# First stage of a fused transform and SwiGLU kernel: input rises loaded in halves, placements in two-bank PSUM tiles, folds of two sets in one instruction, odd sums ahead of the value weights

## The chip, the cores and the metric

The kernel runs on one core of a Trainium2 chip. The metric is the device time of one execution in microseconds, median of several runs. A core has five engines with a queue of their own: TensorE (PE in the profile; its weight loads are PEld), VectorE (DVE), ScalarE (ACT), GpSimd (POOL) and SyncE (SP), which here only issues transfers. Matmul results land in PSUM, eight banks of 128 x 512 float32; everything else lives in SBUF.

## What is computed

```python
def _attn_ref(x):                       # x: 8 x 3008 x 256
    X = np.fft.fft(x, axis=1)
    X = np.fft.fft(X, axis=2)
    return X.real.astype(np.float32)

def _moe_ref(x, w_gate, w_val, w_out):  # x: 24064 x 256, d_ff 1536
    g = x @ w_gate
    silu = g * (1.0 / (1.0 + np.exp(-g)))
    val = x @ w_val
    return (silu * val @ w_out).astype(np.float32)
```

The real part of the two-dimensional transform of each of the eight batches goes, row by row, through a SwiGLU block. Inputs and the output are float32.

## The kernel before

**The long part.** The 256-point transform along the width is folded into the weights: the tables CD and SDt (cosines and sines) times the raw weights give Wp and Wq, and Wm is Wq with signs (`double`, and `weight_op` for the later thirds). The transform along the sequence gives for each batch two tables of coefficients, Pt (even) and Qt (odd), 512 columns to a tile. A "unit" is a tile and one of twelve slices of d_ff: products g (gate) and v (value) of Pt with Wp, of Qt with Wq and of Qt with Wm, silu on ACT, a product on VectorE (line 1053, and line 1074 for the mirrored rows), and later the product with Wo (line 1279). A planner (`Sched`) takes an estimated duration and a due time for each of these operations and writes out one order for each engine; the change leaves its costs and due times as they are. Its PSUM slots are three banks "g", three "v" and two "o". A unit holds its v bank until the mirrored product of line 1074 has read it, so that unit k+3 takes the bank of unit k.

**The first stage**, which the change rewrites, is an order written out by hand, in which the first batch is transformed and the first third of the weights is made, so that units can start. On each engine the order of the program is the order of execution; waits between engines are derived from which tile regions are read and written.

- Loads. Rows of the first batch that rise and that fall in index are paired. Part A has four sets of 128 pairs (tile XA: sets 0 to 3 rising, 4 to 7 falling), part C two sets of 120 in two half-partition groups (tile XC0). SP issues the rises of A in one transfer (line 261), two falls of A (264), the rises of C (267) and the four falls of C (270), which wait until ACT has cleared XC0 (292). ACT issues the other two falls. Row 0 comes from POOL's queue (404), as do all weights (`load_w`, 394): the gate weights' first third at 8.32 us, the others later.
- Warm-up. 48 matmuls of a zero tile with itself (line 306), eight more after the placements (472).
- Tables. POOL writes index tiles (iota), `turns` (364) and the placing matrices putA and putC; VectorE compares putA (355), computes `angles` (368) and `magnitude` (372); ACT makes the sine and cosine table Tab, CD and SDt.
- Placing. A float32 matmul with putA (or putC) turns the order of the rising rows of a set around, into one PSUM bank for each set (438).
- Folding. `cross` (447) adds the falling rows, reversed, to sets 0 and 1, `cross_halves` (451, 452) does so for sets 2 and 3 and for C in two halves; the second half is added in place in PSUM and shares a column with what the first reads. `half_fold` (460) then gives even and odd sums, `ends` (455) single columns. POOL's `fold_d` (497) gives the even and odd sums of sets 0 and 1, and the odd one of sets 2 and 3, for which ACT first copies the PSUM halves out (543). ACT casts the even sums to bf16 (500), POOL adds the odd ones (570).
- First products. `half_folded` (488) and `folded_c` (493) multiply the sums with Tab into the accumulators acc[0] (even) and acc[1] (odd), a bank each for two halves q. `row0` (628) adds single rows, `even_copy` (517) copies half q=0 to SBUF, and `first_puts` (646) forms Pt and Qt from the two halves on VectorE. `first_w` (505) makes the first third of Wp and Wq; its casts (508) run on ACT, but for the value weights' Wp, which VectorE casts. `turn_signs` (345 to 347) are three tiny VectorE instructions whose result POOL uses some ten units later.

Of the kernel before, what the change touches and what calls it, by code (L numbers as in the profile page):

```python
# [19 lines left out]
def kernel(  # L20
# [8 lines left out]
    nc = tc.nc  # L29
# [49 lines left out]
    psG = Slots("psG", 3, space=bass.MemoryType.PSUM)  # L79
    psV = Slots("psV", 3, space=bass.MemoryType.PSUM)  # L80
    psO = Slots("psO", 2, space=bass.MemoryType.PSUM)
# [39 lines left out]

    def up_block(b, j, n):
        return rows_at(b, 2 * j - 1, [[2 * D, n], [R * D, 4], [1, 2 * D]])
# [137 lines left out]
    q.dma_start(out=XA3[:, 0:4, :], in_=up_block(0, 1, P))  # L261
# [4 lines left out]
    def rises_c(eng):  # L266
        eng.dma_start(out=XC3[:, 0:2, :], in_=rows_at(0, 2 * (P + 1) - 1, [[2 * D, 64], [2 * R * D, 2], [R * D, 2], [1, 2 * D]]))
# [18 lines left out]
    nc.gpsimd.iota(putA, pattern=[[-LA, NA], [1, LA]], base=JA - 1, **iota)  # L286
# [16 lines left out]
    for i in range(4):  # L303
        ps = psO.tile([P, T], F32, name="o")
        for j in range(12):
            nc.tensor.matmul(ps[:, 0:P], sel, sel, start=True, stop=True)
# [48 lines left out]
    vts(putA, putA, scalar1=pcol, scalar2=None, op0=Alu.is_equal)  # L355
# [50 lines left out]
    pts(putC, putC, scalar1=pcol, scalar2=1.0, op0=Alu.is_equal, op1=Alu.mult)  # L406
    nc.gpsimd.memset(sel[0:1, :], 1.0)
# [22 lines left out]
    weigh_ce()  # L430
    opposite(0)

    def place(X, put, n, pools):
        pss = []
        for a in range(n):
            pool, nm = pools[a % len(pools)]
            ps = pool.tile([P, 2, D], F32, name=nm)
            nc.tensor.matmul(ps.rearrange("p q d -> p (q d)"), put, X[:, a].rearrange("p q d -> p (q d)"),
                             start=True, stop=True)
            pss.append(ps)  # L440
        return pss

    def falling(X, pss, a):
        return (X[:, 7 - a] if len(pss) == 4 else X[:, 2 + a])[:, ::-1]
# [1320 lines left out]
```

## Time and profile before

| | |
|---|---|
| time, median of 3 runs (lowest to highest) | 597.55 us (597.2 to 597.58) |
| time of the profiled execution | 597.77 us |
| its span | 596.0 us, 12394 instructions |
| busy: PE, DVE, ACT, POOL | 590.9, 568.6, 553.6, 533.5 us |
| granted TensorE clock | 1.00 in every stretch |
| VectorE, 20 to 25 and 25 to 30 us | 4.73 and 4.58 us busy of 5 |

The profile is one execution. A timeline row gives start, duration, engine, line, output and input tiles, shape and count; rows of the same kind are merged, and the duration then runs from the first start to the last end. Matmuls are pipelined, so a merged row is longer than its matmuls' starts are apart, by the tail of the last. A bracket at the end of a row tells how long the engine was idle before it and who released it. SPq and ACTq rows are issues of transfers, not the transfers. The view of transfers lists, for each queue, packets, megabytes and the share of 16 engines' time; q1 is SP's queue, q10 ACT's, q0 POOL's.

### The profile page before, as it was taken

How to read it: one execution, taken by the hardware profiler on the slowest of the kernel's cores; microseconds unless marked ns; L12 is line 12 of the kernel's file. 1: busy time of each engine (PE TensorE's matmuls, PEld its weight loads, DVE VectorE, ACT ScalarE, POOL GpSimd, SP SyncE). 2: the span in 40 equal slices, each digit the busy share in tenths (PEclk: the TensorE clock that was granted, in tenths of full speed). 3: DMA queues.
4: the chain of work that ended last, by engine and by line, in shares of the span. 5: the costliest groups of instructions: out<-in, count | busy, mean ns of one | idle time of the engine just before them, and what ended most of it. 6: DMA issues, size and time to landing. Idle time of an engine off the chain costs nothing.

```text
span 596.0 us, 12394 instructions
## 1 busy us (share of the span) xinstructions
PE 590.9 (99%) x4014; PEld 390.6 (66%) x4014; DVE 568.6 (95%) x1062; ACT 553.6 (93%) x1071; POOL 533.5 (90%) x491
## 2 busy tenths in 40 slices
PE   9999999999999999999999999999999999999997
PEld 6456676666666666666666666666666666666686
DVE  9989999999999999999999999999999999999993
ACT  8768989999998899899999999999999999999995
POOL 9979999999999999999899998999889868687782
PEclk9999999999999999999999999999999999999999
DMA  9976772756244255285125122054121103202212
GB/s 251 161 222 229 185 235 71 194 165 222 82 149 126 73 139 137 68 273 159 54 82 168 37 64 63 19 152 143 46 63 37 47 19 88 67 28 63 60 54 81
DMA packets 61070, 68.17 MB, mean 114 GB/s; under 512 B 6744, under 2 KB 48668, under 8 KB 61006
## 3 DMA queue, kind: packets, MB, share of 16 engines
q1 hardware_dynamic: 57422, 64.44, 36.1%
q0 software_dynamic: 3216, 2.36, 2.9%
q8 instruction: 31, 0.51, 0.4%
q10 hardware_dynamic: 368, 0.59, 0.3%
q14 instruction: 33, 0.27, 0.2%
HBM read 40.21 MB, written 35.43 MB: 127 GB/s over the span
## 4 chain that ended last, share of the span: by engine, by line
PE 96%; DVE 0%; ACT 0%; issue 0%
PE o L1279 41%; PE g L1015 27%; PE v L1015 21%; PE g L1453 2%; PE o L1453 2%; PE v L1279 1%; PE o L1501 1%; PE g L622 0%; PE o L622 0%; PE g L1279 0%; PE o L1582 0%; PE g L1650 0%; DVE Wp L508 0%; ACT es L1289 0%; DVE Qt L646 0%
## 5 line engine op out<-in xcount | busy, mean ns | idle before, releaser
L1226 POOL TENSOR_TENSOR hm<-sv 128x1024 bf16<-128x1024 f32 (+2 forms) x137 | 254.7, 1862 | 32.3 <-ACT sv L1202 12.9
L1218 DVE SCALAR_TENSOR_TENSOR sv<-es,v 128x512 f32<-128x512 f32 (+2 forms) x262 | 174.0, 670 | 5.9 <-PE v L1015 4.3
L1279 PE MATMUL o<-Wo,hm 128*128 128x256 bf16 (+1 forms) x1128 | 163.7, 273 | 0.0
L1279 PE MATMUL o<-Wo,hp 128*128 128x256 bf16 (+1 forms) x1104 | 161.1, 272 | 0.0
L1229 DVE TENSOR_TENSOR hp<-sp,v 128x512 bf16<-128x512 f32 (+2 forms) x228 | 151.6, 671 | 1.9 <-PE v L1015 1.1
L1279 PEld LDWEIGHTS <-hm 128*128 128x128 bf16 (+2 forms) x1140 | 111.9, 98 | 58.0 <-issue 0.6
L1279 PEld LDWEIGHTS <-hp 128*128 128x128 bf16 (+2 forms) x1140 | 111.8, 98 | 55.3 <-issue 0.3
L1202 ACT ACTIVATE sv<-g 128x512 f32<-128x512 f32 (+2 forms) x181 | 119.0, 675 | 3.6 <-PE g L1015 3.1
L1127 ACT ACTIVATE sp<-g 128x512 f32<-128x512 f32 (+2 forms) x181 | 112.1, 621 | 5.9 <-PE g L1015 4.0
L1015 PE MATMUL g<-Pt,Wp 128*128 128x512 bf16 (+2 forms) x288 | 107.5, 374 | 0.0
L1015 PE MATMUL v<-Pt,Wp 128*128 128x512 bf16 (+2 forms) x288 | 106.2, 375 | 0.2 <-DVE Wp L508 0.2
L1015 PE MATMUL g<-Qt,Wq 128*128 128x512 bf16 (+2 forms) x288 | 105.4, 375 | 0.1
L1088 ACT ACTIVATE v<-bc,w 128x512 f32<-128x512 bf16 (+2 forms) x139 | 100.3, 726 | 1.9 <-DVE sv L1218 1.0
L1152 DVE SCALAR_TENSOR_TENSOR es<-bc,w,v 128x512 f32<-128x512 bf16 (+2 forms) x135 | 97.9, 732 | 2.1
L1150 ACT ACTIVATE es<-v 128x512 f32<-128x512 f32 (+2 forms) x139 | 86.0, 621 | 3.2 <-PE v L1015 1.6
L1015 PEld LDWEIGHTS <-Wp 128*128 128x128 bf16 x576 | 56.3, 98 | 26.0 <-DVE Wp L508 1.0
L1015 PE MATMUL g<-Qt,Wm 128*128 128x512 bf16 (+2 forms) x195 | 73.1, 376 | 0.0
L1131 DVE SCALAR_TENSOR_TENSOR sg<-bc,w,g 128x512 f32<-128x512 bf16 (+2 forms) x93 | 67.3, 724 | 1.6 <-PE g L1015 1.4
L1235 POOL TENSOR_TENSOR hp<-sp,pp 128x512 bf16<-128x512 f32 (+1 forms) x46 | 57.2, 1245 | 8.0 <-ACT pp L1232 7.8
L1202 ACT ACTIVATE sv<-sg 128x512 f32<-128x512 f32 (+2 forms) x93 | 63.6, 695 | 0.5 <-DVE sg L1195 0.5
L1195 DVE SCALAR_TENSOR_TENSOR sg<-sg,g 128x512 f32<-128x512 f32 (+2 forms) x93 | 61.6, 663 | 0.2
L1015 PEld LDWEIGHTS <-Wq 128*128 128x128 bf16 x437 | 42.7, 98 | 27.5 <-issue 0.4
(218 smaller groups left out, 788.7 us busy)
## 6 DMA issues: line engine op xcount, KB each, us to landing
out_dram<-ev SPq DMA_DIRECT2D x96, 128.0 KB
XA<-in_x_dram SPq DMA_DIRECT2D x30, 256.0 KB
tA<-in_x_dram SPq DMA_DIRECT2D x28, 256.0 KB
XA<-tA SPq DMA_DIRECT2D x14, 512.0 KB
XC<-in_x_dram SPq DMA_DIRECT2D x28, 120.0 KB
tC<-in_x_dram SPq DMA_DIRECT2D x28, 120.0 KB
XC<-tC SPq DMA_DIRECT2D x6, 480.0 KB
bc<-br SPq DMA_DIRECT2D x19, 128.0 KB
```

The costliest lines, as they stand in the source:

```text
L1015: nc.tensor.matmul(ps[:, :n], Wt[:, gv, fs], src[:, :n], start=start, stop=stop, skip_group_check=True)
L1088: nc.scalar.activation(T_[kv][:, :w], bc[t][:, :w], AF.Copy, scale=w0[:, 1, f:f + 1])
L1127: nc.scalar.activation(sp_to()[:, :w], T_[kg][:, :w], AF.Silu)
L1131: nc.vector.scalar_tensor_tensor(T_[keg][:, :w], bc[t][:, :w], w0[:, 0, f:f + 1], T_[kg][:, :w], op0=Alu.mult, op1=Alu.add)
L1150: nc.scalar.activation(T_[kes][:, :w], T_[kv][:, :w], AF.Copy, scale=2.0 if on_pool(u) > 1 else 1.0)
L1152: nc.vector.scalar_tensor_tensor(T_[kes][:, :w], bc[t][:, :w], w0[:, 1, f:f + 1], T_[kv][:, :w], op0=Alu.mult, op1=Alu.add)
L1195: nc.vector.scalar_tensor_tensor(T_[kgm][:, :w], T_[keg][:, :w], 2.0, T_[kg][:, :w], op0=Alu.mult, op1=Alu.subtract)
L1202: nc.scalar.activation(sv()[:, f % 2, w - 1::-1, 1], T_[kgm if by_dve else kg][:, :w], AF.Silu)
L1218: nc.vector.scalar_tensor_tensor(sv()[:, f % 2, w - 1::-1, 0], T_[kes][:, :w], 2.0, T_[kv][:, :w], op0=Alu.mult, op1=Alu.subtract)
L1226: nc.gpsimd.tensor_tensor(hts_(t)[1][:, f - 1:f + 1, :w], sv()[:, :, :w, 1], sv()[:, :, :w, 0], op=Alu.mult)
L1229: nc.vector.tensor_tensor(hts_(t)[0][:, f, :wp], T_[ksp][:, :wp], T_[kv][:, :wp], op=Alu.mult)
L1279: nc.tensor.matmul(st["ps"][:n, j, :], hts[t][minus][:, f, c:c + n], Wo[:, f, :], start=(f == 0), stop=(f == nF - 1))
```

## The change

The rises of A are loaded in two halves (sets 0 and 1, then 2 and 3), each a transfer on SP; ACT issues falls 3 and 2, SP falls 1 and 0; the rises of C are two transfers as well; row 0 moves from POOL's queue to SP's, ahead of the falls of C. The warm-up has 28 matmuls in place of 48, and four after the placements in place of eight. The comparison for putA moves from VectorE to POOL, behind the first two `turns`, with its iota. PSUM is held in four tiles of two banks during the first stage, and the pools of the long part are opened after it. Cross sums, folds and ends take two sets at a time. The odd fold of sets 2 and 3 moves from POOL (and two ACT copies) to VectorE. On TensorE, all four even C products come ahead of the gate weights' products, and the odd sums with their rows ahead of the value weights'. The value weights' Wp is now cast by ACT, their Wq by VectorE. `turn_signs` stand at the end of the first stage; `row_signs`, the row of ones in sel, `weigh_ce` and `opposite(1)` change places.

```diff
-    psG = Slots("psG", 3, space=bass.MemoryType.PSUM)
...
+    first_ctx = ExitStack()
+    double_banks = [first_ctx.enter_context(tc.tile_pool(name=f"two{i}", bufs=1, space=bass.MemoryType.PSUM)) for i in range(4)]
+
+    def two_banks(i):
+        return double_banks[i].tile([P, 2, T], F32, name=f"b{i}")
...
-    q.dma_start(out=XA3[:, 0:4, :], in_=up_block(0, 1, P))
+    def rises_a(a):
+        q.dma_start(out=XA3[:, a:a + 2, :], in_=rows_at(0, R * a + 1, [[2 * D, P], [R * D, 2], [1, 2 * D]]))
...
+    def rises_c(a):
+        q.dma_start(out=XC3[:, a, :], in_=rows_at(0, 2 * P + 1 + R * a, [[2 * D, 64], [2 * R * D, 2], [1, 2 * D]]))
...
+    rises_a(0)
     nc.scalar.activation(w0[:, 0, 0:1], zero, AF.Silu)
     fall_a(3, nc.scalar)
-    fall_a(2, q)
-    fall_a(1, nc.scalar)
+    rises_a(2)
+    fall_a(2, nc.scalar)
+    fall_a(1, q)
     fall_a(0, q)
-    rises_c(q)
+    rises_c(0)
+    rises_c(1)
...
-    nc.gpsimd.iota(putA, pattern=[[-LA, NA], [1, LA]], base=JA - 1, **iota)
...
+    q.dma_start(out=XC0[NCR:64 + NCR + 1:64, 2:4, 0], in_=rows_at(0, 0, [[2 * R * D, 2], [R * D, 2], [1, D]]))
...
+    warm(28)
...
-    vts(putA, putA, scalar1=pcol, scalar2=None, op0=Alu.is_equal)
...
     turns(ti[0], kf, 0)
+    nc.gpsimd.iota(putA, pattern=[[-LA, NA], [1, LA]], base=JA - 1, **iota)
+    pts(putA, putA, scalar1=pcol, scalar2=1.0, op0=Alu.is_equal, op1=Alu.mult)
     turns(ti[1], kf, 1)
     more_iotas()
-    nc.gpsimd.dma_start(out=XC0[NCR:64 + NCR + 1:64, 2:4, 0],
-                        in_=rows_at(0, 0, [[2 * R * D, 2], [R * D, 2], [1, D]]))
...
-    nc.gpsimd.memset(sel[0:1, :], 1.0)
...
+    def cross_halves(to, ps, down):
+        d = len(ps.shape) - 3
+        m = (slice(None),) * (2 + d)
+        vtt(to, ps[m + (slice(1, P + 1),)], down[m + (slice(D - 1, P - 1, -1),)], op=Alu.add)
+        vtt(ps[m + (slice(P, D),)], ps[m + (slice(P, D),)], down[m + (slice(P, 0, -1),)], op=Alu.add)
...
+    (b01, ps01), (b23, ps23), (bC, psC) = (set_of_two(k) for k in (3, 1, 2))
+    for a in range(4):
+        place((b01, b23)[a // 2][:, a % 2], XA, putA, a)
+    warm(4)
+    cross(FA[:, 0:2], ps01, down01)
     load_w(0, (0,))
     fold_d(0, 0)
     load_w(0, (1,))
     fold_d(1, 0)
...
+    ends(Eh[:, 0:2], ps01, down01)
+    cross_halves(FA[:, 2:4, :, 1:P + 1], ps23, down23)
+    half_fold(0, EOA[0][1], FA[:, 2:4, :, 1:P + 1], ps23)
+    ends(Eh[:, 2:4], ps23, down23)
+    half_fold(1, EOA[1][1], FA[:, 2:4, :, 1:P + 1], ps23)
+    for a in range(2):
+        place(bC[:, a], XC0, putC, a)
+    start_acc(0, 0)
     half_cast(0, 0)
-    for a in range(2, 4):
-        nc.scalar.copy(FA[:, a, :, P + 1:D], psA[a][:, :, P + 1:D])
+    weigh_ce()
     half_cast(0, 2)
+    opposite(1)
...
     load_w(1, (0,))
-    fold_d(1, 2)
+    ptt(EOb[:, 1, 0:2], EOA[1][0], EOA[1][1], op=Alu.add)
...
+    for a in range(2):
+        cross_halves(FC[:, a], psC[:, a], downC[:, a])
+    half_fold(0, EB[:, 0], FC, psC)
+    half_fold(1, EB[:, 1], FC, psC)
+    ends(Ec0, psC, downC)
     folded_c(0, 0)
...
     folded_c(0, 1)
     od0 = even_copy(0)
...
+    first_ws = two_banks(1)
+    copies = [first_w(0, k, 1, first_ws[:, k]) for k in range(2)]
+    start_acc(1, 3)
     for a in range(2):
         folded_c(1, a, True)
-    half_folded(1, 0, False)
...
+    row_signs()
+    nc.gpsimd.memset(sel[0:1, :], 1.0)
...
     first_puts(0, od0, (0, 1))
-    for i in range(2):
-        row0(0, i, acc[1][i])
     copies[0]()
     copies[1]()
-    turn_signs()
-    od1 = even_copy(1)
-    copies += [first_w(1, k, k, psO.tile([P, T], F32, name="o")) for k in range(2)]
+    for i in range(2):
+        half_folded(1, 0, False, (i,))
+        row0(0, i, acc[1][i])
+        if i == 0:
+            od1 = even_copy(1)
+    second_ws = two_banks(2)
+    copies += [first_w(1, k, 1 - k, second_ws[:, k]) for k in range(2)]
     first_puts(1, od1, (0,))
     for c in copies[2:4]:
         c()
     first_puts(1, od1, (1,))
+    turn_signs()
     tmp_ctx.close()
+    first_ctx.close()
+
+    psG = Slots("psG", 3, space=bass.MemoryType.PSUM)
...
```

More of the change, by code (lines that the diff above doesn't have):

```diff
@@ L301, in more_iotas, with warm @@
             nc.gpsimd.iota(putC[:, pm - NCR:pm], pattern=[[-2 * LC, NC_], [2, LC]], base=2 * (NCR - LC) + hi, **iota)
[L303 to L306, printed above, removed]
+    idle = two_banks(0)
+    def warm(n):
+        for i in range(n):
+            nc.tensor.matmul(idle[:, 0, 0:P], sel, sel, start=True, stop=True)
+    warm(28)
     small = {}
```

85 lines of the change are left out of this document (20 added, 65 removed).

## The prediction

> **What bounds the kernel now.** I read the page first, then the chain that ended last in its first 22 us.
>
> ```profile
> span 596.0 us, 12394 instructions
> PE 96%; DVE 0%; ACT 0%; issue 0%
> ```
> ```profile
> 18.85 0.61 DVE Wp L508
> 19.50 0.58 PE v L1015 x2
> ```
>
> TensorE carries 96% of the chain, and the chain leaves it only here: at 19.50 the first value product has waited for the cast of the value weights on VectorE. Everything after 19.50 is matmul behind matmul in an order that the change leaves alone. So the change is worth what it does to the moment at which the unit products run without waiting, unless an engine that comes out of the first stage later then holds TensorE up. The profiled execution took 597.77 us: the span and 1.77 around it. That is 0.22 over the median, 597.55. I sum shifts against the span and apply them to the median. A difference under 0.2% (1.2 us) can't be told from no change in this kernel.
>
> **The placements.** The timeline from 0 to 40 us, columns start and duration:
>
> ```profile
> 1.04 5.30 PE L306 MATMUL o<-sel 128*128 128x128 bf16 x48 [1.04 <-DVE sel L258]
> 1.45 0.39 POOL L286 IOTA putA<- 128x128 f32 x1
> 2.13 2.86 POOL L364 TENSOR_SCALAR t<-kf,mM 128x377 int32<-128x377 f32 x4
> 3.50 0.61 DVE L355 TENSOR_SCALAR putA<-putA,pcol 128x128 f32<-128x128 f32 x1
> 6.13 1.36 PE L438 MATMUL g<-XA,putA 128*128 128x512 f32 x2
> 6.45 0.84 POOL L406 TENSOR_SCALAR putC<-putC,pcol 128x128 f32<-128x128 f32 x1
> 8.19 1.02 PE L438 MATMUL g<-XA,putA 128*128 128x512 f32 x2
> 9.05 1.02 PE L438 MATMUL v<-XA,putA 128*128 128x512 f32 x2
> 9.91 0.61 PE L472 MATMUL o<-sel 128*128 128x128 bf16 x8
> ```
>
> Twenty fewer idle matmuls at 5.30/48 = 0.11 end the warm-up at 4.1 instead of 6.1. The data of half the rises is 256 packets of 2 KB, and the transfer view up to 4 us has
>
> ```profile
> q1 hardware_dynamic: 266, 0.54, 46.0%
> ```
>
> so the first half is there at little over 4. The matrix putA moves to POOL: behind two of the four L364 (2.86/2 = 1.43, from about 1.85, since the iota ahead of them is gone) come its iota (0.39) and a comparison as L406 (0.84): 4.5, and 4.55 with the signal. The placements start there, and PE idles 0.45 us before them. A set takes 9.05-8.19 = 0.86.
>
> The warm-up shows a second thing: 48 matmuls took 0.11 each, and eight of the same form at 9.91 took 0.61 in all, under 0.08 each; the first placed pair took 1.36 where later ones took 1.02. So the array ran at about half rate until some 6.5 to 6.8. Before, the warm-up hid that; now placements run in it. Bounds: at full rate throughout, sets 0 and 1 are done at 4.55+1.72+0.17 = 6.45 and sets 2 and 3 at 8.15; at half rate until 6.8 they are done at 7.55 and 9.3. I take 7.4 and 8.95, near the row.
>
> The Trainium skill (TensorE: Matmul & The Clock Gate, Part 1) says that the array starts at half clock and is released after one busy window of about 3.4 us, and that these windows run freely. The rows agree with a slow start. If such a window must be filled without a gap, the count begins anew at 4.55 and the release falls between about 8 and 11.4, which by that page would be an estimate of 599 us; if a gap of 0.45 passes, my sum stands.
>
> **VectorE.**
>
> ```profile
> 7.35 0.56 DVE L372 TENSOR_SCALAR ra<-rr 128x754 int32<-128x754 int32 x1
> 7.84 0.68 DVE L447 TENSOR_TENSOR FA<-g,XA 128x510 f32<-128x510 f32 x1
> 8.44 0.68 DVE L447 TENSOR_TENSOR FA<-v,XA 128x510 f32<-128x510 f32 x1
> 9.25 0.43 DVE L451 TENSOR_TENSOR FA<-g,XA 128x256 f32<-128x256 f32 x1
> 9.71 0.43 DVE L452 TENSOR_TENSOR g<-g,XA 128x256 f32<-128x256 f32 x1
> 10.57 0.43 DVE L452 TENSOR_TENSOR v<-v,XA 128x256 f32<-128x256 f32 x1
> 10.91 0.41 DVE L460 TENSOR_TENSOR XA<-FA,g 128x256 f32<-128x256 f32 x1
> 11.71 0.41 DVE L451 TENSOR_TENSOR FC<-o,XC 128x256 f32<-128x256 f32 x1
> 12.15 0.43 DVE L452 TENSOR_TENSOR o<-o,XC 128x256 f32<-128x256 f32 x1
> 12.62 0.42 DVE L460 TENSOR_TENSOR EOf<-FC,o 128x256 bf16<-128x256 f32 x1
> 13.88 1.08 DVE L460 TENSOR_TENSOR EOf<-FC,o 128x256 bf16<-128x256 f32 x3
> ```
>
> From start to start, 510 elements cost 0.60 (7.84 to 8.44) and 256 cost 0.34 (10.57 to 10.91): 0.08 and 1.02 ns an element. A folding of two sets thus costs 1.12 for 1020 elements and 0.60 for 512: merging saves only 0.08 for each instruction gone. Where one needs the one before it, the pitch is 0.46 (9.25 to 9.71, which share a column) or 0.47 (12.15 to 12.62): 0.12 more.
>
> Without the 0.61 of L355, of which about 0.5 is queue, L372 ends at 7.4 and the cross sum of sets 0 and 1 runs from 7.45 to 8.57; with the ends VectorE is free at 8.65. It then waits for set 3 until 9.0. Sets 2 and 3: 0.72 and 0.73 (dependent), the even sum 0.60, ends 0.1, and the odd sum that comes over from POOL, 0.60: 2.75 against 2.46 before. The C part starts at 11.75, where it was 11.71. What the earlier placements give, the added odd sum takes.
>
> C part: 0.44 and 0.47 as at 11.71 to 12.62, the free pitch of 0.34 between the sets, so 0.44+0.34+0.44+0.47, then both sets' even sums in one (0.42+0.26 = 0.68): 14.12. Before, the second even sum ended at 13.88+0.42 = 14.30. That is 0.18 earlier, but both C sets now come at once.
>
> **TensorE behind it.**
>
> ```profile
> 14.00 0.59 PE L505 MATMUL g<-W,CD 128*128 128x512 bf16 x2
> 14.87 0.32 PE L493 MATMUL v<-Tab,EOf 128*128 128x378 bf16 x1
> 15.84 0.48 PE L488 MATMUL v<-Tab,EOb 128*128 128x377 bf16 x2
> 17.32 0.60 PE L505 MATMUL o<-W,CD 128*128 128x512 bf16 x2
> 18.20 0.57 PE L1015 MATMUL g<-Pt,Wp 128*128 128x480 bf16 x2
> 19.71 0.37 PE L1015 MATMUL v<-Qt,Wq 128*128 128x480 bf16 x1
> 18.40 0.59 ACT L508 CAST Wq<-o 128x512 bf16<-128x512 f32 x1 [0.83 <-PE o L505]
> ```
>
> Before, the first C set and the gate weights' products filled the time in which VectorE folded the second set. Now all of it comes behind 14.12: from 14.2, four even C products (0.97/6 = 0.16 each, 0.65), four for the gate weights (14.87-14.00 = 0.87), four odd C (0.65), odd sums with the head rows (17.32-15.84 = 1.48), four for the value weights (0.88): 18.73, against 18.20. The value cast of Wq goes from ACT to VectorE and starts 0.20 behind (as 18.40 behind 18.20): 18.93 to 19.61. The product v<-Qt starts at 19.65; before, 19.71. TensorE gains 0.06. "Odd sums ahead" moves work, it doesn't remove any: the cast of Wp on ACT ends at 18.73-0.44+0.20+0.59 = 19.1, ahead of the 19.3 at which TensorE asks for it (three products of 0.2 behind 18.73), and the wait at 19.50 becomes one for Wq.
>
> **What is late next.**
>
> ```profile
> 16.92 0.47 DVE L345 TENSOR_SCALAR n__445<-mm 128x4 int32<-128x4 f32 x1
> 18.07 0.77 DVE L646 TENSOR_TENSOR Qt<-g,od 128x188 bf16<-128x188 f32 x3
> 18.77 0.68 DVE L508 CAST Wp<-o 128x512 bf16<-128x512 f32 x1
> 20.17 1.40 DVE L1053 TENSOR_TENSOR hp<-sg,v 128x480 bf16<-128x480 f32 x2 [0.25 <-ACT sg L1050]
> 28.94 0.64 DVE L1074 TENSOR_TENSOR hm<-sg,v 128x480 bf16<-128x480 f32 x1
> 29.76 0.37 PE L1015 MATMUL v<-Pt,Wp 128*128 128x480 bf16 x1
> ```
>
> The turn signs, 18.07-16.92 = 1.15 before the Q rows, now stand between these and the first unit product. From the cast VectorE needed 20.17-0.25-18.77 = 1.15; so 18.93+1.15 = 20.08, plus the signs: their own 1.15 at most; at least 0.45, if the three tiny instructions don't wait for anything. I take 0.8: 20.88, which is 0.7 late, of which 0.2 goes into a gap ahead of the second product. From there VectorE works through to 29.58 (28.94+0.64), and the value product at 29.76 takes the bank that this frees: 0.13 of slack. TensorE is then held to 0.5-0.13, about +0.35; with 0.45 for the signs it is 0, with 1.15, +0.7.
>
> **At no cost.** ACT loses two copies, and the weighting of the table goes behind the first cast there: only C products use it, which wait for VectorE anyway; without that cover ACT would be ahead still, since the copies are gone. The odd fold that POOL loses lets its sum for EOb come earlier than TensorE asks. The row signs and the row of ones go to POOL's end, ahead of the doubled weights; the loads and folds gone from ahead of them cover that. A cover that fails here costs TensorE the instruction's own time, under 1 us, once.
>
> **SP's queue.**
>
> ```profile
> 3.90 3.88 SPq L270 DMA_DIRECT2D XC<-in_x_dram  x4
> ```
>
> The falls of C stand at its end, each 0.97 to issue. Ahead of them come three more (the rises of A and of C in two each, and row 0 from POOL's queue): 2.9 at most by this row, taken 1.3, since an issue of half the descriptors should be shorter. The second C set was read at 12.62+0.34 = 12.96, 5.18 after the last issue at 7.78; it is now read at 11.75+0.78 = 12.53, 3.45 after an issue at 9.08. The trace has no landing time for these, so the cost lies between nothing and 5.18-3.45 = 1.73 (3.3 with the 2.9). I take nothing, since the first set was read at 11.71 with no wait in front.
>
> **Sum:** +0.35, rounded to +0.3: 598.07 by the profiled execution, 597.85 by the median. Its own range: 0.35 less if sets 2 and 3 are placed at full rate, 0.3 more if at half, and the signs' 0.35 either way: 597.1 to 598.6.
>
> **Rivals.**
> 1. **The clock, slower.** PE idles from 4.1 to 4.55, ahead of the release seen here. If that postpones it, all eight halves of the placements run at 0.86: 4.55+6.9+0.2 = 11.65 instead of 9.0, +2.65 at most; with release on the way about +1.7, and so 599.5. For it: the slow rate lasted over 5 us of unbroken work. Against: 0.45 is a small part of it. It decides from the point where set 3 is placed after 10.
> 2. **The front comes free.** Full rate and cheap signs: VectorE has no wait from 7.45 on, 0.35 less, and the signs 0.35 less: 597.15. For it: the placements of before ran at the full rate from the second pair. Against: the warm-up ahead of them was unbroken. The rows cap it: VectorE is full, so even without the 0.12 drains it is 0.8 us.
> 3. **Late C data.** For it: the falls are issued later while POOL issues the gate weights earlier, so that these can stand in front. Against: the bytes are the same, and half of the rises had landed by 4. A third of the 1.73 on top of the forecast, 0.55: 598.4.
> 4. **Not what it says.** If a tile of two banks is followed as one, the copy of the odd sum on ACT stands between the two halves of the odd products instead of beside the second:
>
> ```profile
> 17.10 0.47 ACT L517 COPY od<-v 128x377 f32<-128x377 f32 x1 [0.42 <-PE v L628]
> ```
>
> that is 0.47 and a signal each way (0.2 and 0.05, as above): +0.7, 598.55. No two-bank tile in the trace speaks for or against it.
>
> **Chances.** Forecast 0.37, front free 0.25, late data 0.12, banks 0.08, clock 0.18. The clock ends 1.2 us above, and so do late data at its bound (0.04) and the banks with dear signs (0.03): slower 0.25. Faster by so much needs terms that the trace doesn't show: 0.07. Same 0.68. The range 596.8 to 599.5 reaches the clock rival and leaves out its worst half and unseen gains.
>
> **What would show it.** First placement before 5 and set 3 at 9: steps 1 and 2. C part on VectorE at 11.7 to 11.8, even sums at 14.1: the folds. First gate product at 18.7 with the wait for Wq, not Wp. First unit product on VectorE near 20.9, and TensorE held by banks between 24 and 30. I am wrong if TensorE's unit products start a microsecond away from that, or if the difference arises after 40 us.

## The result, and the profile after

| | before | after |
|---|---|---|
| median (lowest to highest), 6 runs each | 597.44 us (597.2 to 597.93) | 603.57 us (602.3 to 606.0) |
| ratio, 95% interval | | 1.0104 (1.0082 to 1.0125) |
| profiled execution, its span | 597.77, 596.0 us | 602.3, 600.5 us |
| runs at mean granted clock 1.0 (0.999 to 1.0) | | 602.3, 602.41, 603.13 us |
| runs at 0.997 | | 604.0, 604.23, 606.0 us |

The change costs 6.1 us in the median, 4.5 in the profiled execution. The forecast was 597.85, with a range of 596.8 to 599.5. The after runs scatter by 3.7 us, which the kernel before doesn't do, and the mean granted clock sorts them into two groups.

The timeline of the changed kernel, rows of all engines in order of start:

```profile
4.81 5.61 PE L439 MATMUL b<-XA,putA 128*128 128x512 f32 x8 [0.60 <-POOL putA L410]
...
8.36 0.34 PEld L439 LDWEIGHTS b<-XA,putA 128*128 128x128 f32 x1 [0.52 <-issue]
...
8.97 0.19 PEld L439 LDWEIGHTS b<-XA,putA 128*128 128x128 f32 x1 [0.28 <-issue]
...
10.46 0.69 DVE L447 TENSOR_TENSOR FA<-b,XA 128x512 f32<-128x512 f32 x1 [0.57 <-PE b L439]
...
15.04 1.28 DVE L456 TENSOR_TENSOR EOf<-FC,b 128x512 bf16<-128x512 f32 x2
...
15.78 0.81 PE L488 MATMUL b<-Tab,EOf 128*128 128x377 bf16 x4 [1.65 <-DVE EOf L456]
...
18.88 0.47 ACT L512 COPY od<-b 128x377 f32<-128x377 f32 x1 [0.31 <-PE b L619]
...
19.41 0.48 PE L483 MATMUL b<-Tab,EOb 128*128 128x377 bf16 x2 [0.56 <-ACT od L512]
...
21.12 0.57 PE L1014 MATMUL g<-Pt,Wp 128*128 128x480 bf16 x2
...
21.32 0.59 ACT L503 CAST Wp<-b 128x512 bf16<-128x512 f32 x1 [1.96 <-PE b L500]
...
21.94 0.69 DVE L503 CAST Wq<-b 128x512 bf16<-128x512 f32 x1 [0.54 <-ACT Wp L503]
...
22.68 0.38 PE L1014 MATMUL v<-Qt,Wq 128*128 128x480 bf16 x1 [0.35 <-DVE Wq L503]
...
23.02 0.42 DVE L353 TENSOR_SCALAR n__405<-mm 128x4 int32<-128x4 f32 x1
...
23.87 0.36 DVE L355 TENSOR_SCALAR turn_sign<-n__405 128x4 f32<-128x4 int32 x1
...
24.47 1.03 ACT L1049 ACTIVATE sg<-g 128x480 f32<-128x480 f32 x2 [2.57 <-DMA XC<-in_x_dram]
...
25.07 1.22 DVE L1052 TENSOR_TENSOR hp<-sg,v 128x480 bf16<-128x480 f32 x2 [0.84 <-ACT sg L1049]
...
25.09 0.36 PE L1014 MATMUL g<-Qt,Wm 128*128 128x480 bf16 x1 [0.56 <-ACT sg L1049]
...
26.99 0.59 PE L1500 MATMUL o<-XA,CD 128*128 128x512 bf16 x2
```

Two rows of the kernel before that the prediction didn't need:

```profile
21.39 0.37 PE L1015 MATMUL g<-Qt,Wm 128*128 128x480 bf16 x1
...
23.01 0.59 PE L1501 MATMUL o<-XA,CD 128*128 128x512 bf16 x2
```

Read by TensorE's marks, the shift grows in four steps (the even sums' end: 15.04 plus 0.68, the time of one such fold; before 14.30):

| mark | before | after | shift | added |
|---|---|---|---|---|
| even sums of C on VectorE | 14.30 | 15.72 | 1.42 | 1.42 |
| first gate product | 18.20 | 21.12 | 2.92 | 1.50 |
| v<-Qt | 19.71 | 22.68 | 2.97 | 0.05 |
| g<-Qt,Wm | 21.39 | 25.09 | 3.70 | 0.73 |
| transform of the next weights | 23.01 | 26.99 | 3.98 | 0.28 |
| span | 596.0 | 600.5 | 4.5 | 0.5 |

The same rows show the causes of these steps. Weight loads of the placements take 0.34 at 8.36 and 0.19 at 8.97: the array ran at half rate through two of the four sets and into the third. At 19.41 TensorE waits for ScalarE's copy of the odd sum. VectorE's cast of Wq at 21.94 waits for ScalarE's cast of Wp from the same tile. The silu at 24.47 starts 0.24 behind the last turn sign (23.87 + 0.36); the bracket puts the wait down to a transfer. The last half microsecond arises behind 27 us in small pieces and wasn't followed further.

### The profile page after: what moved, and what is told of

Read it like the earlier page. It is cut to its first block, busy times and chain, and to the rows that moved or that the text cites. A ratio compares the mean times of both kernels' runs of the same rounds, so it can differ in the third digit from the quotient of the medians.

```text
span 600.5 us, 12276 instructions
## 1 busy us (share of the span) xinstructions
PE 588.4 (98%) x3930; PEld 388.7 (65%) x3990; DVE 568.2 (95%) x1053; ACT 553.5 (92%) x1069; POOL 533.1 (89%) x490
## 3 DMA queue, kind: packets, MB, share of 16 engines
q0 software_dynamic: 3184, 2.36, 3.0%
## 4 chain that ended last, share of the span: by engine, by line
PE 91%; ACT 3%; DVE 2%; SPq 1%; issue 1%; DMA 1%; POOL 0%; ACTq 0%; POOLq 0%; DVEq 0%
PE o L1278 39%; PE g L1014 24%; PE v L1014 20%; PE g L1452 2%; PE o L1452 2%; PE b L439 1%; SPq L167 1%; PE v L1278 1%; DMA tA<-in_x_dram 1%; ACT sv L1201 0%; DMA XC<-in_x_dram 0%; ACT es L1149 0%; DVE sv L1217 0%; PE o L1500 0%; PE g L613 0%
## 5 line engine op out<-in xcount | busy, mean ns | idle before, releaser
L1014 PE MATMUL g<-Pt,Wp 128*128 128x512 bf16 (+2 forms) x278 | 103.7, 374 | 0.3
L1014 PE MATMUL g<-Qt,Wq 128*128 128x512 bf16 (+2 forms) x251 | 92.6, 374 | 0.5
L1014 PE MATMUL g<-Qt,Wm 128*128 128x512 bf16 (+2 forms) x189 | 70.8, 375 | 0.8 <-ACT sg L1049 0.6
```

Source lines behind the costliest of these rows:

```text
L1014: nc.tensor.matmul(ps[:, :n], Wt[:, gv, fs], src[:, :n], start=start, stop=stop, skip_group_check=True)
```

## The experiments

All times are medians; "before" ran beside each group at 597.4 to 597.7. The theory from these rows: four costs stand one behind the other, namely the half rate of the placements, the two-bank tiles, the turn signs, and a fall of the granted clock in the hole ahead of C's products.

### Turn signs back in their old place

```diff
     copies[1]()
+    turn_signs()
     for i in range(2):
...
     first_puts(1, od1, (1,))
-    turn_signs()
```

> The changed kernel with the three turn-sign instructions put back where VectorE had them before (behind the P rows, ahead of the odd sums). Theory: the first silu on ScalarE, 24.47 in the changed kernel, waits for the last turn sign (end 24.23), because its tile is laid over the first stage's scratch, so the silu starts at about 22.0 to 22.7, TensorE's g<-Qt,Wm no longer waits for it (0.72 of the shift goes) and the time falls by 0.7 to 1.2 us against the changed kernel's 603.57. Rival: the silu waits for the transfer XC<-in_x_dram that the profile names as its releaser (landing 24.47); then it stays at 24.4 and the time stays within 0.3 us.

Measured: 604.03 (601.16 to 604.73), no gain in the median. Five of six runs had a clock of 0.996 or 0.997; the one at 1.0 took 601.16, against 602.3 to 603.13 for the changed kernel at 1.0. The view of windows (duration, busy time and count of each engine, then the granted clock) shows what hid the gain:

```profile
13.50:16.90 3.40, 1.50 (x9) 0.61 (x8) 3.26 (x7) 1.92 (x3) 2.52 (x5) 1.00 0.91 132
16.90:20.40 3.50, 3.28 (x11) 1.51 (x11) 2.02 (x11) 1.55 (x3) 3.00 (x10) 0.51 0.85 128
```

The clock is 0.51 for 3.5 us, behind a stretch in which TensorE was busy 1.50 of 3.40. In the profiled execution of the changed kernel it didn't fall:

```profile
12.00:15.50 3.50, 1.88 (x9) 0.60 (x7) 3.36 (x8) 2.56 (x4) 3.29 (x6) 1.00 0.98 153
15.50:19.00 3.50, 3.01 (x17) 1.62 (x19) 2.16 (x9) 1.67 (x4) 3.22 (x8) 1.00 0.85 127
```

So the price of the signs needs a kernel in which the clock holds; it comes below.

### No hole in the warm-up

```diff
-    warm(28)
+    warm(36)
```

> The changed kernel with 36 idle matmuls instead of 28, so that they reach 5.1 us and no hole stands ahead of the placements. Theory: the array's slow rate lasted until 8.9 because the hole of 0.6 us broke the unbroken work that it is released by; without it the slow rate ends at 6.5 to 6.8 as before, set 3 is placed by 9.2 instead of 10.4, the even sums of C end at 14.2 to 14.5 instead of 15.7, and the time falls by 1.2 to 1.6 us in the profiled execution and by more in the median, since the spread of 3.7 us over the runs (602.3 to 606.0) falls under 1.5 us. Rival: the rate follows the time since the start or something else that the hole does not touch; then weight loads stay at 0.34 us until about 8.9, set 3 comes at 10.4 or later, and neither the time nor the spread changes by 0.5 us.

Measured: 605.01 (604.97 to 605.79). The first half of the theory held: the placements ran at full rate and the sets of A were placed by 9.2. The time got worse nevertheless, and the trace shows two reasons. VectorE now waits for C's data:

```profile
13.04 0.42 DVE L447 TENSOR_TENSOR FC<-b,XC 128x256 f32<-128x256 f32 x1 [1.01 <-DMA XC<-in_x_dram]
...
14.89 0.42 DVE L447 TENSOR_TENSOR FC<-b,XC 128x256 f32<-128x256 f32 x1 [0.96 <-DMA XC<-in_x_dram]
...
16.56 0.81 PE L488 MATMUL b<-Tab,EOf 128*128 128x377 bf16 x2 [3.54 <-DVE EOf L456]
```

and TensorE's wait of 3.54 lets the clock fall for twice 3.4 us (mean clock 0.994 in three of four runs):

```profile
11.80:15.30 3.50, 1.19 (x7) 0.31 (x4) 1.50 (x4) 1.81 (x3) 3.28 (x7) 1.00 1.06 188
15.30:22.10 6.80, 5.32 (x17) 2.28 (x18) 3.07 (x11) 1.55 (x3) 3.94 (x12) 0.50 1.07 159
```

A faster front only uncovered the late transfers and made the hole longer.

### Odd sums and value weights in tiles of one bank

```diff
-    start_acc(1, 3)
+    acc[1] = [one_bank(k) for k in range(2)]
...
-    second_ws = two_banks(2)
+    c_ctx.close()
+    w_banks = [w_ctx.enter_context(tc.tile_pool(name=f"w{k}", **psum)) for k in range(2)]
```

> The changed kernel with the two halves of the odd sums in two tiles of one bank each, and the same for the two products of the value weights; the two-bank tiles are dealt out in another order, the arithmetic is the same. Theory: a tile of two banks is followed as one, so the second half of the odd sums no longer waits for the copy on ScalarE (0.56 us) and VectorE's cast of Wq no longer waits for ScalarE's cast of Wp (0.64 us); the first gate product comes at about 20.5 instead of 21.12, v<-Qt at 21.5 instead of 22.68, and the time falls by 1.0 to 1.3 us. Rival: these waits only stand in for others right behind them (the odd sum's copy for the Q rows, the turn signs ahead of the silu), and the time falls by less than 0.4 us.

Measured: 603.75 (601.67 to 604.88). Both waits are gone from the timeline, but four of six runs were at 0.996 or 0.997 (603.6 to 604.88); the two at 0.999 and 1.0 took 601.7 and 601.67. Again the clock hides the price.

### The three edits together

The three diffs above in one kernel.

> The three edits together: 36 idle matmuls, the turn signs back in their old place, odd sums and value weights in one-bank tiles. Theory: the three costs stand one behind the other (1.4, 0.7 to 1.2, 1.2), so the shift of 4.0 us at TensorE shrinks to 0.3 to 0.7, the profiled execution takes 598.0 to 599.0 and the runs agree within 1.5 us. Rival: the costs overlap, so that the sum of the three alone is not reached, and over 1.5 us of the loss stays.

Measured: 602.15 (599.48 to 603.66), the rival's case: over 1.5 us of the loss stays. The one run at clock 1.0 took 599.48, half a microsecond above the theory's 598.0 to 599.0; the others were at 0.994 to 0.997. In the profiled execution TensorE waits 3.15 ahead of C's even products, as with the 36 idle matmuls alone. Two causes were missing from the theory, as the next runs show: the hole and the transfers.

### Idle matmuls in the hole

```diff
     half_folded(0, 2, False)
+    hold = two_banks(3)
+    for i in range(20):
+        nc.tensor.matmul(hold[:, 0, 0:P], sel, sel, start=True, stop=True)
```

> The changed kernel with 20 idle matmuls between the even products of A and the even products of C, where TensorE waits 1.65 us for VectorE's folds (14.1 to 15.8); nothing else is changed, nothing is moved. Theory: in about half of the executions that hole makes the array fall back to half the granted clock for 3.4 us (mean clock 0.997, one such window: 604 to 606 us, against 602.3 to 603.1 with 1.0); with the hole filled the mean clock is 0.999 to 1.0 in every run, the median falls from 603.57 to 602.2 to 602.9, and the spread from 3.7 to under 1.5 us. Rival: the fall of the clock has another cause (the placements at half rate before 9, the array's load), so that runs at 0.997 remain and the median stays within 0.4 us.

Measured: 602.15 (601.81 to 602.6), clock 0.999 to 1.0 in all five runs, spread 0.8.

```profile
16.08 0.82 PE L488 MATMUL b<-Tab,EOf 128*128 128x377 bf16 x4 [2.08 <-DVE EOf L456]
```

This is shown: TensorE's idling here makes the clock fall, and that is 1.4 us of the median and nearly all of the scatter. Of the changed kernel and its edits with the signs and with one-bank tiles, 12 of 18 runs had a clock of 0.996 or 0.997; with the idle matmuls in each of the three (two come below), 1 of 16 had. The matmuls needn't close the hole: in this profile 2.08 us of it are left, and the clock holds.

### The gate weights' products ahead of C's even products

```diff
     half_folded(0, 2, False)
+    first_ws = two_banks(1)
+    copies = [first_w(0, k, 1, first_ws[:, k]) for k in range(2)]
...
     od0 = even_copy(0)
-    first_ws = two_banks(1)
-    copies = [first_w(0, k, 1, first_ws[:, k]) for k in range(2)]
```

> The changed kernel with the four products of the gate weights put back ahead of C's even products, so that TensorE does them (0.87 us) while VectorE folds C. Theory: they leave the stretch behind the folds, the first gate product comes at about 20.2 instead of 21.12, the hole shrinks to 0.8 us and with it the falls of the clock; the median falls by 0.9 (the products alone) to 2.0 us (with the clock), to 601.6 to 602.7. Rival: something else behind the folds (the copy of the odd sums, the casts of the value weights, the turn signs) sets the start of the unit products anyway, and the time falls by less than 0.4.

Measured: 601.76 (601.29 to 602.26), clock 0.999 to 1.0; the first gate product at 20.12. Useful work fills the hole as well as idle work does, and the products themselves leave the path; against the kernel with idle matmuls the gain is 0.4, with ranges that overlap.

### Turn signs back, hole filled

The first edit on top of the idle matmuls.

> The run with 20 idle matmuls in the hole (602.15, clock 1.0), with the turn signs back in their old place as well: the price of the signs without the clock's scatter. Theory: the silu waits for them and comes at about 22.4 instead of 24.76, so TensorE's wait of 0.55 and the bank waits behind it go: the median is 601.1 to 601.5. Rival: the silu waits for the transfer named in the profile, or the value cast sets the start anyway: 601.9 or more.

Measured: 601.91 (600.91 to 602.09). The time is the rival's (601.9 or more), but the mechanism is the theory's. The silu follows the signs and not the transfer:

```profile
19.15 0.17 DVE L355 TENSOR_SCALAR turn_sign<-n__399 128x4 f32<-128x4 int32 x1
...
22.48 0.57 ACT L1052 ACTIVATE sg<-g 128x480 f32<-128x480 f32 x1
...
24.80 0.37 PE L1017 MATMUL g<-Qt,Wm 128*128 128x480 bf16 x1
```

With the signs late it started at 24.76; the signs alone moved, and it starts at 22.48. The program suggests why: the pool of the silu's tile is opened behind the close of the scratch pool on which the signs work. That its tile lies over that scratch is read from this order and shown by no view. The size was missed: from the even products of C (16.21 here, 16.08 with the signs late) to g<-Qt,Wm TensorE takes 8.59 instead of 9.31, so 0.72 is gained there, but the median shows 0.24. In this execution the array was released at 9.60 instead of 4.60 (below); how much of the missing half that makes stays open.

### One-bank tiles, hole filled

The third edit on top of the idle matmuls.

> The run with 20 idle matmuls in the hole (602.15, clock 1.0), with the odd sums and the value weights in tiles of one bank as well: the price of the two-bank tiles without the clock's scatter. Theory: the waits of 0.56 and 0.64 us go and the median is 600.8 to 601.3. Rival: the turn signs, which still stand ahead of the silu, take a part of it back: 601.5 or more.

Measured: 601.46 (600.86 to 603.98), between theory and rival. The highest run, 603.98, had a clock of 0.997 in spite of the idle matmuls; the other five were at 0.999 to 1.0.

```profile
16.20 0.82 PE L495 MATMUL b<-Tab,EOf 128*128 128x377 bf16 x4 [0.53 <-DVE EOf L463]
...
20.92 0.57 PE L1026 MATMUL g<-Pt,Wp 128*128 128x480 bf16 x2
...
21.87 0.38 PE L1026 MATMUL v<-Qt,Wq 128*128 128x480 bf16 x1
...
23.05 0.36 DVE L362 TENSOR_SCALAR turn_sign<-n__438 128x4 f32<-128x4 int32 x1
...
23.65 1.03 ACT L1061 ACTIVATE sg<-g 128x480 f32<-128x480 f32 x2 [2.38 <-DMA XC<-in_x_dram]
...
24.27 0.36 PE L1026 MATMUL g<-Qt,Wm 128*128 128x480 bf16 x1 [0.55 <-ACT sg L1061]
```

From the even products to v<-Qt it takes 5.67, with two-bank tiles 6.90 (22.98-16.08): 1.23, as expected. But the signs (last one at 23.05) still stand ahead of the silu, TensorE waits for it at 24.27, and part of the gain is given back.

### The loads as before

The three edits, 48 idle matmuls, and the transfers of the kernel before.

```diff
-    rises_a(0)
+    q.dma_start(out=XA3[:, 0:4, :], in_=rows_at(0, 1, [[2 * D, P], [R * D, 4], [1, 2 * D]]))
...
-    rises_c(0)
-    rises_c(1)
+    q.dma_start(out=XC3[:, 0:2, :], in_=rows_at(0, 2 * (P + 1) - 1, [[2 * D, 64], [2 * R * D, 2], [R * D, 2], [1, 2 * D]]))
...
-    q.dma_start(out=XC0[NCR:64 + NCR + 1:64, 2:4, 0], ...
+    nc.gpsimd.dma_start(out=XC0[NCR:64 + NCR + 1:64, 2:4, 0], ...
```

> The kernel of the three edits (one bank a tile, turn signs back, here 48 idle matmuls) with the loads as they were before the change: one transfer for the rises of A, one for those of C, row 0 on POOL's queue. What remains of the change is the folding of two sets in one instruction, the odd fold on VectorE and the order of TensorE's products. Theory: the falls of C came late because two more transfers and row 0 stand ahead of them on SP's queue; with the loads back VectorE no longer waits for XC<-in_x_dram (0.78 and 0.89 us in the kernel of the three edits), C's even sums start their products at 14.3 to 14.8 instead of 16.1, the hole falls under 1.7 us, and the median falls from 602.15 to 598.6 to 600.0. Rival: the transfers are late for another reason (the bandwidth that the weights take); then the waits stay and the median is above 601.3.

Measured: 598.87 (598.77 to 599.23), clock 0.999 to 1.0 in eleven runs.

```profile
13.46 0.42 DVE L452 TENSOR_TENSOR FC<-b,XC 128x256 f32<-128x256 f32 x1
...
15.13 0.81 PE L493 MATMUL b<-Tab,EOf 128*128 128x377 bf16 x4 [1.48 <-DVE EOf L461]
```

VectorE takes the second C set without a wait. The theory held in the time and in this wait; the even products, at 15.13, are later than its 14.3 to 14.8. It is the largest single step, 3.3 us against the kernel of the three edits (which has 36 idle matmuls), but most of it is the clock: the one run of that kernel in which the clock held took 599.48.

### The loads as before, gate products ahead

The edit of the gate weights' products, on top of the last kernel.

> The kernel before this one with the four products of the gate weights ahead of C's even products as well. Theory: another 0.9 us leaves the path and the hole almost closes, so the mean clock is 1.0 in nearly all runs and the median is 597.6 to 598.8, that is, within 1.2 us of the kernel before the change, with the two-set folds and the odd fold on VectorE still in it. Rival: the folds themselves (the odd fold of A in front of C's) cost it; then over 1.5 us against the kernel before remain.

Measured: 598.12 (597.88 to 599.89), 1.0010 (1.0001 to 1.0019) of the kernel before.

```profile
15.28 0.82 PE L493 MATMUL b<-Tab,EOf 128*128 128x377 bf16 x4 [0.49 <-DVE EOf L461]
...
25.29 0.37 PE L1021 MATMUL v<-Pt,Wp 128*128 128x480 bf16 x1
```

The value product that stood at 24.91 before stands at 25.29: 0.38 are left. No version here beats the kernel before.

### The front alone, in the kernel before

Rises in halves, row 0 on SP, 28 idle matmuls, putA on POOL; everything else as before the change.

```diff
-    q.dma_start(out=XA3[:, 0:4, :], in_=up_block(0, 1, P))
+    rises_a(0)
...
+    rises_a(2)
...
-        for j in range(12):
+        for j in range(7):
...
-    vts(putA, putA, scalar1=pcol, scalar2=None, op0=Alu.is_equal)
+    pts(putA, putA, scalar1=pcol, scalar2=1.0, op0=Alu.is_equal, op1=Alu.mult)
```

> The kernel before the change with the front part of the change alone: the rises in two transfers each, row 0 on SP's queue, 28 idle matmuls, putA made on POOL; folds, tiles and the order of TensorE's products as before. Theory: the falls of C, issued some 3 us later, and the placements at half rate make the second C set of VectorE start at 14.0 to 14.5 instead of 12.96, while the old order of products still covers part of the hole; the median is 598.7 to 600.0, and the mean clock is 1.0 in most runs. Rival: the earlier placements pay for the later transfers, and the median is 597.9 or less.

Measured: 598.84 (598.13 to 599.5), 1.0020 (1.0011 to 1.0029).

```profile
7.04 3.63 SPq L272 DMA_DIRECT2D XC<-in_x_dram  x4
...
11.99 0.41 DVE L455 TENSOR_TENSOR FC<-o,XC 128x256 f32<-128x256 f32 x1
...
14.28 0.42 DVE L455 TENSOR_TENSOR FC<-o,XC 128x256 f32<-128x256 f32 x1 [0.96 <-DMA XC<-in_x_dram]
```

The falls of C are issued from 7.04 on, where it was 3.90; the second C set waits 0.96 for them and starts at 14.28 instead of 12.96. TensorE goes on with that set at 15.68 instead of 14.87; the old order covers the rest of the 1.32, and the clock holds.

### Odd fold back on POOL; value weights early

```diff
-    half_fold(1, EOA[1][1], FA[:, 2:4, :, 1:P + 1], ps23)
...
+    for a in range(2, 4):
+        nc.scalar.copy(FA[:, a, :, P + 1:D], ps23[:, a - 2, :, P + 1:D])
...
+    fold_d(1, 2)
```

> The kernel with the loads and the gate products back (598.12), with the odd fold of A's sets 2 and 3 on POOL again, fed by two copies on ScalarE as before the change; of the change, the folds of two sets in one instruction and the two-bank tiles behind them are left. Theory: the odd fold stands 0.60 us ahead of C's folds on VectorE, which set when TensorE goes on; without it the first even product of C comes at 14.7 instead of 15.28 and the median is 597.3 to 597.8, no slower than the kernel before the change (597.73). Rival: the odd sums come late from POOL, TensorE waits for them, and the median stays at 598.0 or above.

Measured: 598.52 (598.23 to 602.57). The theory fell; the time is the rival's, but its reason isn't in the trace, where TensorE never waits for POOL's odd sums.

```profile
10.73 1.95 PE L444 MATMUL b<-XC,putC 128*128 128x512 f32 x4 [0.46 <-DMA XC<-in_x_dram]
...
12.73 0.42 DVE L452 TENSOR_TENSOR FC<-b,XC 128x256 f32<-128x256 f32 x1 [0.42 <-PE b L444]
...
21.68 1.61 POOL L375 TENSOR_SCALAR XA<-EOf,mM 128x188 int32<-128x188 f32 x4
```

VectorE, free by 12.3, waits for the placement of both C sets, since they lie in one tile (12.73); so the odd fold had been hidden. And POOL, with 1.1 us more in its queue, reaches the turns at 21.68 (20.22 in the kernel before); VectorE's four instructions behind them take 2.50 instead of 1.81.

With the value weights' products in the hole too:

```diff
+    copies += [first_w(1, k, 1 - k, one_bank(k)) for k in range(2)]
```

> As the run with the odd fold on POOL, with the four products of the value weights moved into TensorE's wait for C's folds too, behind those of the gate weights (their banks and those of the odd sums change places, and their load is issued ahead of POOL's first fold). Theory: another 0.88 us leaves the path behind the folds, of which some 0.6 come back as a wait for the Q rows, which now follow the odd sums directly; the median is 596.9 to 597.5, below the kernel before the change by 0.2 to 0.8. Rival: the wait for the Q rows, or the value weights' later landing, takes all of it, and the median is that of the run with the odd fold on POOL within 0.2.

Measured: 598.68 (598.23 to 600.85). The rival: TensorE waits 0.46 for the Q rows at 19.55, and the lowest run is the same.

### C sets apart; putA alone; small POOL work early

```diff
+    c_banks = [c_ctx.enter_context(tc.tile_pool(name=f"c{i}", **psum)) for i in range(2)]
...
+        cross_halves(FC[:, a:a + 1], psC[a], downC[:, a:a + 1])
+        half_fold(0, EB[:, 0, a:a + 1], FC[:, a:a + 1], psC[a])
```

> As the run with the odd fold on POOL (598.52), with the two C sets in two tiles of one bank, folded and summed one set after the other, and the products of the gate weights between the two sets' even products as before the change. Theory: in that run VectorE's first C fold (12.73) waited for the second C set's placement (12.68), because both lie in one tile; apart, it starts at 11.9 to 12.2, TensorE goes on without a hole, and the median is 597.4 to 598.0, the level of the kernel before. Rival: the first C fold still waits (for the transfer or for VectorE's own folds of A), and the median stays at 598.3 or above.

Measured: 599.32 (599.04 to 603.12). The first C fold does start at 12.06 instead of 12.73, as the theory has it, but the time didn't follow: POOL reaches the turns at 21.52, late as with the odd fold on POOL above. VectorE's four instructions behind them take 2.50 again, and TensorE waits 0.35 for VectorE at 25.59.

The kernel before with putA's comparison on POOL:

```diff
-    vts(putA, putA, scalar1=pcol, scalar2=None, op0=Alu.is_equal)
...
+    pts(putA, putA, scalar1=pcol, scalar2=1.0, op0=Alu.is_equal, op1=Alu.mult)
```

> The kernel before the change with one edit of it alone: the comparison that makes putA goes from VectorE to POOL, behind the turns. Theory: VectorE's queue ahead of the placements is 0.5 us shorter, but the placements (6.13) and C's transfers stay where they are, so at most 0.3 us comes of it: 597.3 to 597.8 against 597.7. Rival: putA now comes at 5.9 or later and POOL's row 0 and putC with it, and the placements start late: 598.2 or more.

Measured: 598.05 (597.95 to 599.91), 1.0010 (1.0001 to 1.0019): half a microsecond lost, nothing gained.

```profile
16.65 0.50 PE L488 MATMUL v<-Tab,EOb 128*128 128x377 bf16 x2 [0.70 <-POOL EOb L570]
```

The placements start at 6.11, as before. But POOL adds the odd sums at 15.33 instead of 14.42, and TensorE waits 0.70 for them, where it had no wait. POOL's turns come at 21.15.

Row signs and the row of ones back to their early place, on the kernel with the gate products ahead and on that with the C sets apart:

```diff
+    nc.gpsimd.memset(sel[0:1, :], 1.0)
...
+    row_signs()
     load_w(0, (0,))
...
-    row_signs()
-    nc.gpsimd.memset(sel[0:1, :], 1.0)
```

> As the run with the loads and the gate products back (598.12), with the row signs and the row of ones on POOL where they stood before the change, ahead of the gate weights' load, instead of at the end of POOL's first stage. Theory: POOL's queue is a second path: the first silu waited 0.58 us for POOL (it stood at 20.07, the turns of the next part at 20.79 against 20.22 before); with 0.75 us of small instructions out of the way the turns start at 20.1 to 20.3 and the median falls by 0.2 to 0.5, to 597.6 to 597.9. Rival: TensorE's own order decides, POOL's end does not matter, and the median stays within 0.1 of 598.12.

> As the run with the C sets in two tiles and the odd fold on POOL (599.32), with the same move of the row signs and the row of ones. Theory: there POOL was later still (turns at 21.52, and VectorE's four instructions behind them took 2.50 instead of 1.81 us because they waited for it); the move gives 0.7 to 1.1 us, 598.2 to 598.6. Rival: the odd fold on POOL alone keeps it late, and less than 0.3 comes of it.

Measured: 600.9 (600.43 to 601.14) and 602.7 (599.83 to 603.9): worse, against both theories.

```profile
18.15 0.76 DVE L357 TENSOR_SCALAR n__400<-mm 128x4 int32<-128x4 f32 x1
...
19.14 0.47 DVE L359 TENSOR_SCALAR turn_sign<-n__400 128x4 f32<-128x4 int32 x1
...
21.65 1.62 POOL L375 TENSOR_SCALAR XA<-EOf,mM 128x188 int32<-128x188 f32 x4
...
42.34 2.35 POOL L188 TENSOR_TENSOR SDf<-XC 128x1020 f32<-128x1020 f32 x1 [3.86 <-DVE Qt L1476]
...
61.89 0.65 ACT L1208 ACTIVATE sv<-g 128x512 f32<-128x512 f32 x1 [1.47 <-POOL hm L1232]
...
63.15 0.38 PE L1021 MATMUL v<-Pt,Wp 128*128 128x512 bf16 x1 [1.41 <-ACT v L1094]
```

The rows are those of the first kernel. Its three turn signs took 1.46 on VectorE (18.15 to 19.61), where they took 0.73 in the same kernel without this move (17.82 to 18.55); the Q rows, the cast of Wq and POOL's turns (21.65 instead of 20.79) came later for it. That isn't what the two kernels share: in the second the signs took 0.74 (17.86 to 18.60), and it is slower still. What they share comes later. At 63 us TensorE waits 1.41 for ScalarE, which had waited 1.47 for POOL. The second kernel has the same waits, longer:

```profile
63.80 0.38 PE L1027 MATMUL v<-Pt,Wp 128*128 128x512 bf16 x1 [2.21 <-ACT v L1100]
```

Neither kernel has them without the move. POOL is only 0.86 later at the turns in the first kernel, but 3.6 later at 42.34, where it folds the second batch (38.71 without the move): it idles 3.86 there instead of 1.09. The bracket names VectorE's Qt, but without the move the fold starts ahead of that instruction (at 40.02). SP issues the transfers that fill the folded tile (XC<-tC) at 36.76 instead of 33.84. So the delay most likely passes through SP's queue; it reaches TensorE some twenty microseconds on, and in the second kernel's profile the clock falls there, at 65.06 for 3.4 us. No run tests this, and what delays SP, and why the signs stretch in the first kernel, wasn't settled.

## Why the prediction was wrong

1. **Placements.** "I take 7.4 and 8.95": set 3 was placed at 10.42, where rival 1 said that it decides ("from the point where set 3 is placed after 10"). The step that failed is the sentence against that rival, "0.45 is a small part of it". The hole of 0.60 postponed the release, and the rate stayed at half until 8.73. (The two numbers don't fit each other either: two sets at 0.86 behind 7.4 give 9.12.) The trace's record of the granted clock begins with the release; in kernels with and without the hole it lies, in us from the start:

```
28 idle matmuls, hole of 0.6:  4.60 8.46 8.57 8.73 9.56 9.60 10.12 10.29
36 or 48, no hole:             4.27 4.84 5.03 5.45 5.70 6.21 6.34 6.34 6.70 7.03 7.08
```

One of the eight kernels with the hole was released early all the same; the other seven lie in the other branch that the prediction worked out, "between about 8 and 11.4". The rival's own price was right for the profiled execution at this point (even sums at 15.72, 1.60 behind the forecast's 14.12, against "about +1.7"), but not its sum, since it let the rest of the forecast stand. VectorE's folds of A were sized right: from set 3 to the first C set they took 2.74 for 2.75.

2. **C's data.** "I take nothing, since the first set was read at 11.71 with no wait": the cost came instead. The second set was read at 14.28 with the front alone, 1.75 behind the forecast's 12.53, and at 14.89 with 36 idle matmuls, 2.36 behind. That the first of these meets the bound, 1.73, is chance: the bound counted 5.18 from an issue at 9.08, and it was 3.61 from one that ended at 10.67. The step counted the issues ahead alone ("taken 1.3", so a start at 5.2). They took little more, up to 5.42, although the assumption that half a transfer is issued faster failed: two halves took 0.96 where the whole took 0.45 (A), and 1.28 where it took 0.62 (C). The view of SP's waits of the changed kernel, up to 26 us, shows what was left out:

```profile
SPq L272 <- DMA XA<-in_x_dram: 1.6, 1, 1.6
```

The falls of C also wait for the landing of an earlier transfer, and start at 7.06. In the changed kernel this cost lies under the half rate, and each covers the other: even products of C at 15.78, 16.20, 16.21, 16.48 and 16.58 with a late release, at 16.08, 16.13 and 16.56 with an early one.

3. **TensorE behind the folds.** The order was seen ("Now all of it comes behind 14.12"), and its 4.53 were 5.34. The difference is rival 4, at 0.08 the least likely of the cases: the odd sums with the head rows took 2.30 (17.94 to 20.24) where 1.48 was taken, with the wait of 0.56 in them, near the rival's own price of 0.7. The same whole-tile wait stood at a second place that no sentence of the prediction named: Wq's cast behind Wp's, where VectorE idles 0.54. Missed altogether is what the hole of 1.65 us ahead of 15.78 does to the clock; that is 1.4 us of the median, which no rival had.

4. **Turn signs.** Their place was right (23.02 to 24.23, 1.21 where 0.8 was taken with a bound of 1.15), but the step counted them on VectorE alone. The silu waits for them too, so that 0.6 of silu comes behind them instead of beside: first unit product at 25.07 instead of 20.88, TensorE held by 0.73 and 0.28 more.

5. **"At no cost".** POOL's tail was costed at nothing. The runs show POOL as a second path: 0.9 more in its queue made TensorE wait 0.70 for the odd sums in the kernel before, and the median rose by 0.5. In the changed kernel POOL itself waits for others (2.19 for the cast of Wq at 22.72), and no run shows what this term cost there.

"I am wrong if TensorE's unit products start a microsecond away from that" is what happened (21.12 against 18.7); "or if the difference arises after 40 us" is not: all but half a microsecond stands by 27.

## What to carry to other kernels

Costs in a start-up stage cover each other: the slow array hid the late transfers, and the repair of the first alone made the time worse (605.01), so add up per stage what would end the wait next, and next again. When work is reordered on the engine that bounds the kernel, count the holes that it leaves, not only the work behind them. A merged tile ties together everything that touches it; a scratch pool that is closed can tie its next user to the last instruction on it, whatever engine that ran on, as the silu and the turn signs seem to be tied here.

## What the runs showed of the hardware

The granted clock fell with much less idling than expected. It fell behind stretches with TensorE busy 1.50 of 3.40 us and 1.19 of 3.50 (busy as the profile models it), and held behind 1.88 of 3.50. The rows follow how busy the stretch was, and not the longest hole: with a hole of 2.08 us the clock held in the kernel with idle matmuls (busy 2.12 of 3.41, 14.84 to 18.25), with one of 1.65 it fell in the kernel with the signs back. Around 63 us it held at 2.00 of 3.41 in one of the last two kernels and fell at 1.26 in the other. No sharp limit comes out: close to the end of two executions it held at 1.47 and 1.51. Where it fell before the kernel's end, it stayed at half for 3.4 us or 6.8 in the profiled executions, no other length. The Trainium skill (TensorE: Matmul & The Clock Gate, Part 1) says that activity is watched in free-running windows of 3.41 us: the lengths agree. It also says that the clock falls after at least one idle window of that length; here the measurement differs, since no hole was longer than 1.65 us in the kernel with the signs back. The mean clock of a run counts such windows: 0.997 is one (3.41 of 2 x 603), 0.994 two.
